# Seven block products for the down product of the last two FFN blocks, in place of whole tiles, with their output stored transposed

## The chip, the core and the metric

The kernel runs on one core of a Trainium2 chip. The metric is the device time of one execution in microseconds (us), as the median of several runs. Beside it stands one execution taken with the hardware profiler: its own time, the span from its first to its last instruction, and its trace. PE is TensorE, DVE VectorE, ACT ScalarE, POOL GpSimd, SP the engine that issues the DMAs.

## The reference

Attention with two kinds of masks over 4 batches gives 2304 tokens of width 512. A mixture of experts follows (MoE: 8 experts, each 512 to 1024 to 512, relu, gates from a Sinkhorn iteration), then an FFN (512 to 2048 to 512) whose activation is the sigmoid form of gelu. The change concerns the FFN alone:

```python
def _moe2_ref(x, w_in, w_out) -> np.ndarray:
    h = x @ w_in
    g = h * (1.0 / (1.0 + np.exp(-1.702 * h)))
    return (g @ w_out).astype(np.float32)
```

All matrices are float32. The kernel multiplies in a reduced format (fp32r) and keeps the precision by splitting each operand into a high and a low part: three matmuls (high by high, high by low, low by high) make one product.

## The kernel before

**Blocks, phases, units.** The tokens form three blocks of 768 (`BT`; half of one is `NH` = 384). There are six phases: MoE on blocks 0, 1, 2, then FFN on blocks 0, 1, 2. A phase is cut into units of 256 hidden columns: 32 units in a MoE phase, 8 in an FFN phase. Units are numbered through: 0 to 31, 32 to 63, 64 to 95 are the MoE phases, 96 to 103, 104 to 111, 112 to 119 the FFN phases. `S0` = 32 is the first unit of MoE block 1, `S1` = 96 the first FFN unit.

**Up product.** Each unit multiplies its token block by its 512x256 weights in a 2x2 block scheme with seven products instead of eight (Winograd's form; the table `PRODUCTS`). A product is six matmuls of 128x128 by 384 columns, so a unit has 42 of them. They go into PSUM banks A, B, C. ACT copies (`pB<-pA`, `c<-pC`, `c<-pA`) and DVE additions between the products finish the four quarters "11", "12", "21", "22" of the hidden block.

**Down product, by whole tiles.** In MoE block 0 and in all FFN blocks, `activate` makes for each quarter a high part `hh` and a low part `hl`. For the FFN that is a chain of four instructions: ACT sigmoid `sg`, DVE product `sg`, ACT copy `hh`, DVE difference `hl`. One unit later `tile_down` multiplies: six token tiles of 128, six matmuls of 512 columns each, 36 in a unit, and DVE adds each tile to the sums `acc`. Products and tiles alternate on PE. Quarter "12" comes from the last but one product of a unit and is wanted by the first tile in the next unit.

**Down product, by seven block products.** In MoE blocks 1 and 2 (`seven(i)`) the down product uses the same 2x2 scheme over a pair of units. `scaled` finishes a quarter `r`, `down_input_sum` forms four sums `s` on POOL, and `combination` and `low_part` split all seven inputs into high (ACT) and low parts in the tiles `comb`. The seven weight blocks come from DRAM (`sw7`, tiles `w7`), made once in MoE block 0. `chain` multiplies: 14 chains for a pair, each six matmuls of 384 columns, so 42 matmuls for a unit, two units later than the up products. DVE adds each chain to the sums `sums7`. The result is transposed (features by tokens), which is the form in which the FFN wants it.

**Weights.** The FFN weights come as 64-bit numbers and are decoded in the MoE phases (`plan_decode`). `plan_ahead` makes the sums and the split parts of three FFN units there already (its tiles are `ws`, its stores go to `s1ffn` and `s2ffn`). The other five units' parts are made while FFN block 0 runs, by ACT (high) and POOL (low), and stored for blocks 1 and 2.

**Order.** Everything is written in one order by hand: a unit is a row of pieces (product, down tile, product, ...), and lists of side work (`side`) hang on the pieces. Each engine executes its own instructions strictly in that order.

Of the kernel before, what the change touches and what calls it, by code (L numbers as in the profile page):

```python
# [15 lines left out]
P = 128  # L16
# [13 lines left out]
AHEAD = 3  # L30
# [27 lines left out]
def strided_attention_moe_ffn(  # L58
# [58 lines left out]
    sw2 = dram.tile([UF, 2, P, 2 * D], F32, name="s2ffn")  # L117
    sw7 = dram.tile([E * UPE, NPR, P, D], F32, name="s7moe")
# [168 lines left out]
    def split_w1(i, k):  # L287
# [20 lines left out]

    def split_w2(i, ft):
# [7 lines left out]
        kept = [(kept, f(t))] if kept is not None else []
        if kind == "moe":

            for k, (_, what, *_) in enumerate(PRODUCTS):  # L320
                if what[0] == "W" and int(what[1]) == ft + 1:
                    c = (int(what[2]) - 1) * D
                    kept.append((sw7[n, k], f(t)[:, c : c + D]))
# [1307 lines left out]
```

## Time and profile before

| what | value |
|---|---|
| median of 3 runs | 1961.44 us (1958.18 to 1962.76) |
| the profiled execution's own time | 1956.79 us |
| its span | 1955.0 us |
| PE busy | 1919.4 us, 98% of the span |
| DVE, ACT, POOL busy | 74%, 44%, 64% |
| granted PE clock, mean | 0.994 of full speed |
| DMA | 545.75 MB, 279 GB/s |

The profiled execution lies 4.65 us below the median of the runs, and its time is 1.8 us more than its span. Matmuls overlap each other in the profile, so a busy PE is not by itself a PE at its peak. What a stage costs is read from how many matmuls a stretch of it holds.

### The profile page before, as it was taken

How to read it: one execution, taken by the hardware profiler on the slowest of the kernel's cores; microseconds unless marked ns; L12 is line 12 of the kernel's file. 1: busy time of each engine (PE TensorE's matmuls, PEld its weight loads, DVE VectorE, ACT ScalarE, POOL GpSimd, SP SyncE). 2: the span in 40 equal slices, each digit the busy share in tenths (PEclk: the TensorE clock that was granted, in tenths of full speed). 3: DMA queues.
4: the chain of work that ended last, by engine and by line, in shares of the span. 5: the costliest groups of instructions: out<-in, count | busy, mean ns of one | idle time of the engine just before them, and what ended most of it. 6: DMA issues, size and time to landing. Idle time of an engine off the chain costs nothing.

```text
span 1955.0 us, 34399 instructions
## 1 busy us (share of the span) xinstructions
PE 1919.4 (98%) x11276; PEld 1793.0 (92%) x11276; DVE 1455.9 (74%) x2751; ACT 864.3 (44%) x2152; POOL 1242.0 (64%) x1249
## 2 busy tenths in 40 slices
PE   6999999999999999999999999999999999999999
PEld 5777888898888999999999999999999998888888
DVE  4787778777766788788878788888886766756555
ACT  4555556676665333333333433333333445533332
POOL 3456666777777677677777888888887767600100
PEclk8999999999999999999999999999999999999999
DMA  5457779999997898888898888999988867665653
GB/s 213 152 209 270 266 276 331 385 338 350 379 330 248 318 307 290 297 286 283 285 303 286 253 310 293 341 327 322 364 314 314 294 222 265 237 189 187 222 192 121
DMA packets 283649, 545.75 MB, mean 279 GB/s; under 512 B 30832, under 2 KB 51536, under 8 KB 282576
## 3 DMA queue, kind: packets, MB, share of 16 engines
q1 hardware_dynamic: 283184, 543.09, 80.5%
q8 instruction: 91, 1.49, 0.3%
q14 instruction: 86, 0.70, 0.1%
q10 hardware_dynamic: 288, 0.47, 0.1%
HBM read 381.90 MB, written 161.53 MB: 278 GB/s over the span
## 4 chain that ended last, share of the span: by engine, by line
PE 80%; DVE 2%; POOL 1%; ACT 0%; issue 0%; DMA 0%; ACTq 0%; DVEq 0%
PE y L1177 22%; PE pA L1017 22%; PE pC L1017 11%; PE y L1284 6%; PE y L1283 6%; PE y L1282 6%; PE pB L1017 5%; DVE xs L552 0%; POOL s L1149 0%; POOL comb L1124 0%; DVE comb L1124 0%; POOL xc L568 0%; DVE xc L572 0%; DVE r L1130 0%; DMA w<-s1moe 0%
## 5 line engine op out<-in xcount | busy, mean ns | idle before, releaser
L1017 PE MATMUL pA<-xc,w 128*128 128x384 f32 x2880 | 572.3, 336 | 1.9 <-DVE pB L1072 1.9
L1177 PE MATMUL y<-comb,w 128*128 128x384 f32 x2688 | 537.6, 334 | 1.4 <-DVE sum L1187 1.4
L1017 PEld LDWEIGHTS pA<-xc,w 128*128 128x128 f32 x2880 | 508.0, 188 | 18.8 <-DVE pB L1072 2.9
L1177 PEld LDWEIGHTS y<-comb,w 128*128 128x128 f32 x2688 | 472.0, 188 | 2.5 <-DVE sum L1187 2.4
L1124 POOL TENSOR_TENSOR comb<-s,comb 128x384 fp32r<-128x384 f32 x256 | 283.3, 1117 | 89.1 <-ACT comb L1119 82.4
L1187 DVE TENSOR_TENSOR sum<-y,sum 128x384 f32<-128x384 f32 x420 | 231.4, 552 | 98.5 <-PE y L1177 96.8
L1017 PE MATMUL pC<-xc,w 128*128 128x384 f32 x1464 | 295.0, 336 | 0.0
L1017 PEld LDWEIGHTS pC<-xc,w 128*128 128x128 f32 x1464 | 258.6, 188 | 10.0
L1284 PE MATMUL y<-w,hl 128*128 128x512 f32 x672 | 266.9, 397 | 0.4 <-DVE hl L1056 0.4
L1282 PE MATMUL y<-w,hh 128*128 128x512 f32 x672 | 263.4, 392 | 3.7 <-DVE acc L1297 2.0
L1283 PE MATMUL y<-w,hh 128*128 128x512 f32 x672 | 265.3, 395 | 0.0
L1119 ACT ACTIVATE comb<-r 128x384 fp32r<-128x384 f32 x192 | 101.0, 526 | 364.0 <-DVE r L1130 348.3
L252 POOL TENSOR_TENSOR w<-raw,w 128x512 fp32r<-128x512 f32 (+1 forms) x100 | 117.6, 1182 | 74.4 <-ACT w L258 69.9
L1284 PEld LDWEIGHTS y<-w,hl 128*128 128x128 f32 x672 | 125.9, 187 | 28.3 <-DVE hl L1056 1.0
L1282 PEld LDWEIGHTS y<-w,hh 128*128 128x128 f32 x672 | 126.2, 188 | 22.8 <-DVE acc L1297 2.6
L1017 PE MATMUL pB<-xc,w 128*128 128x384 f32 x708 | 142.4, 335 | 0.0
L1283 PEld LDWEIGHTS y<-w,hh 128*128 128x128 f32 x672 | 126.0, 187 | 15.9
L1124 POOL TENSOR_TENSOR comb<-r,comb 128x384 fp32r<-128x384 f32 x64 | 67.5, 1054 | 114.4 <-ACT comb L1119 114.4
L1119 ACT ACTIVATE comb<-s 128x384 fp32r<-128x384 f32 x256 | 131.5, 514 | 11.0 <-POOL s L1149 10.9
L1149 POOL TENSOR_TENSOR s<-r,r 128x384 f32<-128x384 f32 x127 | 134.8, 1082 | 2.1 <-DVE r L1130 2.0
L1311 DVE TENSOR_TENSOR acc<-y,acc 128x512 f32<-128x512 f32 x126 | 86.8, 689 | 63.3 <-PE y L1284 63.1
L1017 PEld LDWEIGHTS pB<-xc,w 128*128 128x128 f32 x708 | 125.2, 188 | 4.7
(178 smaller groups left out, 2878.0 us busy)
## 6 DMA issues: line engine op xcount, KB each, us to landing
w<-s1moe SPq DMA_DIRECT2D x448, 256.0 KB, 4.9
w<-s7moe SPq DMA_DIRECT2D x448, 256.0 KB, 4.9
s1moe<-w SPq DMA_DIRECT2D x216, 256.0 KB, 4.5
w<-s1ffn SPq DMA_DIRECT2D x133, 256.0 KB, 2.7
s7moe<-kw SPq DMA_DIRECT2D x116, 256.0 KB, 4.9
s7moe<-w SPq DMA_DIRECT2D x96, 256.0 KB, 4.7
w<-s2ffn SPq DMA_DIRECT2D x38, 512.0 KB, 3.7
raw<-wa SPq DMA_DIRECT2D x32, 512.0 KB, 5.9
```

The lines of the kernel that those rows point to most:

```text
L252: eng.tensor_tensor(out=t[:, 1], in0=src, in1=f(high), op=ALU.subtract)
L1017: nc.tensor.matmul(out=o, lhsT=w[:, hw, kk * P : (kk + 1) * P], rhs=x[:, hx, kk, :], start=opens and m == 0, stop=ends and m == len(todo) - 1,
L1119: nc.scalar.activation(out=t[:, 0, :], in_=part[i, q], func=AF.Copy)
L1124: eng.tensor_tensor(out=t[:, 1, :], in0=part[i, q], in1=f(t[:, 0, :]), op=ALU.subtract)
L1149: eng.tensor_tensor(out=part[i, q], in0=part[i, a], in1=part[i, b], op=op)
L1177: nc.tensor.matmul(out=o, lhsT=t[:, hw, dt * P : (dt + 1) * P], rhs=x[:, hx, :], start=(n == 0), stop=(n == 5))
L1187: nc.vector.tensor_tensor(out=a, in0=o, in1=a, op=ALU.add)
L1282: nc.tensor.matmul(out=o, lhsT=hh[:, c], rhs=w[:, 0], start=(m == 0), stop=False)
L1283: nc.tensor.matmul(out=o, lhsT=hh[:, c], rhs=w[:, 1], start=False, stop=False)
L1284: nc.tensor.matmul(out=o, lhsT=hl[:, c], rhs=w[:, 0], start=False, stop=(m == 1))
L1311: nc.vector.tensor_tensor(out=a, in0=y, in1=a, op=ALU.add)
```

## The change

FFN blocks 1 and 2 (units 104 to 119) get their down products by `chain` over pairs of units, as MoE blocks 1 and 2 have them. FFN block 0 keeps its tiles. `scaled` gets a branch for the FFN: ACT sigmoid `sg`, DVE product `r`. The sums of blocks 1 and 2 are joined and stored by `join_parts` and `store_part`, features by tokens, and the host puts the transposed part back. The weight blocks for this (`sw7["ffn"]`) are made for four units in the MoE phases (`AHEAD` = 4; two of them now in MoE block 1) and for the other four in FFN block 0, where their low parts and those of three of the seven up blocks go to DVE. On DVE the high part is staged, so ACT copies it twice. The whole-tile weights `sw2` are kept for the four early units alone.

```diff
-AHEAD = 3
+AHEAD = 4
...
+    F1 = FIRST_UNIT[NB + 1]
+    RANGES = ((S0, S1), (F1, NU))
 
     def seven(i):
-        return S0 <= i < S1
+        return any(lo <= i < hi for lo, hi in RANGES)
...
-            split_into(t, src, kept, store=2 if i > PLAIN else 0)
+            split_into(t, src, kept, nc.vector if kind == "ffn" and k % 2 else nc.gpsimd, store=2 if i > PLAIN else 0)
...
-        eng, tag = (nc.gpsimd, "sums") if again is None else (nc.vector, "psums")
+        ffn = UNITS[i][1] == "ffn"
+        eng, tag = (nc.gpsimd, "dsums" if ffn else "sums") if again is None else (nc.vector, "psums")
+        low = nc.vector if ffn else eng
+        last = i in (S0 - 1, F1 - 1)
...
-            split_into(t, src, sw7[n, k].rearrange("p (h c) -> p h c", h=2), eng, 1, 3)
+            split_into(t, src, sw7[UNITS[i][1]][n, k].rearrange("p (h c) -> p h c", h=2), low, 1, 3)
...
+            def down_sum(m, r=r):
+                w, t = r["raw"].rearrange("p (q c) -> p q c", q=4), r["sums"]
+                a, b = (
+                    (w[:, 1], w[:, 0]), (w[:, 3], w[:, 1]), (w[:, 3], t[:, 0, :]), (w[:, 2], t[:, 2, :])
+                )[m]
+                nc.gpsimd.tensor_tensor(out=t[:, m, :], in0=a, in1=b, op=ALU.subtract)
+
+            def split_down(k, m, r=r, n=n):
+                kept = sw7["ffn"][n, k].rearrange("p (h c) -> p h c", h=2)
+                src = r["sums"][:, WHERE[PRODUCTS[k][1]][1], :]
+                split_into(half_of(r, m).bitcast(F32R), src, kept, low=1, store=3)
...
+            tasks += [lambda m=m, down_sum=down_sum: down_sum(m) for m in range(4)]
+            tasks += [lambda k=k, m=m, fn=split_down: fn(k, m) for k, m in ((1, 0), (2, 1), (4, 0), (6, 1))]
+            tasks += [lambda: None] * 2
...
+        if UNITS[i][1] == "moe":
+            half = rows[UNITS[i][2], UNITS[i][3] // UPE][:, (int(q[0]) - 1) * NH : int(q[0]) * NH]
+            nc.vector.scalar_tensor_tensor(out=t, in0=src, scalar=0.0, in1=half, op0=ALU.max, op1=ALU.mult)
+        else:
+            sg = stp.tile([P, NH], F32, tag="sg", name="sg", bufs=2)
+            nc.scalar.activation(out=sg, in_=src, func=AF.Sigmoid, scale=1.702)
+            nc.vector.tensor_tensor(out=t, in0=src, in1=sg, op=ALU.mult)
...
+    def order_of(u):
+        return (0, 1, 2, 4, 5, 3, 6) if u == NU - 2 else tuple(range(NPR))
...
+    def store_part(ph, n, h):
+
+        half, dt = divmod(n, 2)
+        blk = UNITS[FIRST_UNIT[ph]][2]
+        o = out[blk * BT : (blk + 1) * BT, :].rearrange("t d -> (t d)").rearrange("(k p t) -> k p t", p=P, t=BT)
+        src = sum_of(ph, DOWN.index(PARTS[n]))[:, h, :]
+        nc.sync.dma_start(out=o[2 * dt + h, :, half * NH : (half + 1) * NH], in_=src)
+
+    def join_parts(ph, a, b, h, eng, stored=None):
+
+        o, x = (sum_of(ph, DOWN.index(q))[:, h, :] for q in (a, b))
+        eng.tensor_tensor(out=o, in0=o, in1=x, op=ALU.add)
+        if stored is not None:
+            store_part(ph, stored, h)
...
+            last = {
+                2: [(v, "12", "11", 0)],
+                3: [(g, "S4", "S1")],
+                4: [(v, "S2", "11"), (v, "S3", "S2"), (g, "S4", "S2")],
+                5: [(v, "22", "S3", 2), (g, "S1", "S3", 3)],
+            }
+            for k, steps in last.items():
+                side[piece_at(NU, k)] += [join(h, *step) for step in steps for h in range(2)]
...
-        plan_ahead(piece_at(FIRST_UNIT[2] + 5, 0), piece_at(S1 - 4, 0))
+        M2 = FIRST_UNIT[2]
+        ends = [(S0 + 11, S0 + 19), (S0 + 19, M2 - 4), (M2 + 5, M2 + 17), (M2 + 17, S1 - 4)]
+        plan_ahead([(piece_at(lo, 0), piece_at(hi, 0)) for lo, hi in ends])
...
-    return r.results[0]["y"]
+    y = r.results[0]["y"]
+    t = y[BT:].reshape(-1, _OUTS[0][1], BT).transpose(0, 2, 1)
+    return np.concatenate([y[:BT], t.reshape(-1, _OUTS[0][1])])
```

**PE, inside an FFN unit of block 2.** Before, one product (L1017) stands between two down tiles of six 512-column matmuls (L1282 to L1284); the numbers behind `w_`, `hh_` are buffers.

```order
L1282 MATMUL y<-w_23230,hh_23318 128x512
L1283 MATMUL y<-w_23230,hh_23318 128x512
L1284 MATMUL y<-w_23230,hl_23319 128x512
L1282 MATMUL y<-w_23254,hh_23274 128x512
L1283 MATMUL y<-w_23254,hh_23274 128x512
L1284 MATMUL y<-w_23254,hl_23275 128x512
L1017 MATMUL pA<-xc,w_23289 128x384 x6
```

Now a product (L1040) is followed by one chain (L1211), three matmuls for each unit of the pair:

```order
L1040 MATMUL pA<-xc,w_23699 128x384 x6
L1211 MATMUL y_23917<-comb_23623,w_23778 128x384 x3
L1211 MATMUL y_23917<-comb_23802,w_23778 128x384 x3
L1040 MATMUL pA<-xc,w_23763 128x384 x6
L1211 MATMUL y_23945<-comb_23623,w_23778 128x384 x3
L1211 MATMUL y_23945<-comb_23802,w_23778 128x384 x3
```

The 512-column matmuls are gone from units 104 to 119, and the two inputs of a chain (`comb`) belong to units that are one and two units older.

**ACT, across the end of unit 102 (FFN block 0).** These are the instructions from the fourth product's quarter "11" to quarter "12", before; `w` are split up-weights, `xc<-z` an input for the next block.

```order
L1061 ACTIVATE sg<-pB 128x384
L1063 ACTIVATE hh_20832<-sg 128x384
L258 ACTIVATE w_20838<-raw_20721 128x2x256
L258 ACTIVATE w_20851<-sums 128x256
L1061 ACTIVATE sg<-pB 128x384
L1063 ACTIVATE hh_20864<-sg 128x384
L258 ACTIVATE w_20880<-sums 128x256
L563 ACTIVATE xc<-z 128x768
L1061 ACTIVATE sg<-pC 128x384
L1063 ACTIVATE hh_20892<-sg 128x384
```

Now, from the fourth of these rows on:

```order
L259 ACTIVATE w_21004<-sums 128x256
L259 ACTIVATE kw<-dsums 128x256
L269 ACTIVATE high<-dsums 128x256
L1084 ACTIVATE sg<-pB 128x384
L1086 ACTIVATE hh_21020<-sg 128x384
L259 ACTIVATE kw<-dsums 128x256
L269 ACTIVATE high<-dsums 128x256
L259 ACTIVATE w_21040<-sums 128x256
L586 ACTIVATE xc<-z 128x768
L259 ACTIVATE kw<-dsums 128x256
L269 ACTIVATE high<-dsums 128x256
L1084 ACTIVATE sg<-pC 128x384
```

Three pairs `kw`, `high` (the new down-weight parts) stand between, two of them behind the sigmoid of quarter "22" and ahead of that of quarter "12".

**DVE, at the very end.** Before, the last rows are quarter "21" of the last unit and the additions of the last tiles:

```order
L1062 TENSOR_TENSOR sg<-pA,sg 128x384
L1311 TENSOR_TENSOR acc<-y,acc 128x512
L1066 TENSOR_TENSOR hl_23451<-sg,hh_23450 128x384
L1311 TENSOR_TENSOR acc<-y,acc 128x512 x5
L1627 UNCONDITIONAL_BRANCH
```

Now there are additions of chains (L1221, `sum<-y,sum`) and joins of two sums (L1238); each `y` is one chain.

```order
L1238 TENSOR_TENSOR sum_23040<-sum_23040 128x384 x2
L1221 TENSOR_TENSOR sum_23260<-y_24168,sum_23260 128x384
L1221 TENSOR_TENSOR sum_23260<-y_24176,sum_23260 128x384
L1221 TENSOR_TENSOR sum_23260<-y_24189,sum_23260 128x384
L1221 TENSOR_TENSOR sum_23260<-y_24197,sum_23260 128x384
L1238 TENSOR_TENSOR sum_23260<-sum_23260,sum_23040 128x384 x2
L1238 TENSOR_TENSOR sum_23040<-sum_23040,sum_23260 128x384 x2
L1221 TENSOR_TENSOR sum_23040<-y_24214,sum_23040 128x384
L1221 TENSOR_TENSOR sum_23040<-y_24222,sum_23040 128x384
L1238 TENSOR_TENSOR sum_23040<-sum_23040 128x384 x2
L1221 TENSOR_TENSOR sum_23260<-y_24238,sum_23260 128x384
L1221 TENSOR_TENSOR sum_23260<-y_24247,sum_23260 128x384
```

Of the last 14 chains, which follow each other on PE without a product between them, the first row stands between the additions of the sixth and the seventh. Four joins now stand between the additions of the tenth and the eleventh chain, and two more in front of the last two additions.

## Rows read from the trace of the kernel before

**Rows 1.** The page's head and part 1: busy us, share of the span, instructions.

```profile
span 1955.0 us, 34399 instructions
PE 1919.4 (98%) x11276; PEld 1793.0 (92%) x11276; DVE 1455.9 (74%) x2751; ACT 864.3 (44%) x2152; POOL 1242.0 (64%) x1249
```

**Rows 2.** Waits of PE from 315 us on: total us, times, longest.

```profile
PE pA L1017 <- DVE pB L1072: 1.9, 3, 1.0
PE y L1177 <- DVE sum L1187: 1.4, 3, 0.8
PE y L1282 <- ACT hh L1063: 1.1, 1, 1.1
PE ptr L989 <- DVE pr L980: 0.6, 1, 0.6
```

**Rows 3.** Stretches: length, busy us (instructions) of PE, PEld, DVE, ACT, POOL; clock, DMA, GB/s.

```profile
641.71:651.65 9.94, 9.94 (x67) 9.75 (x67) 3.82 (x8) 6.54 (x13) 6.76 (x7) 1.00 0.75 223
797.25:1044.77 247.52, 247.52 (x1429) 247.52 (x1429) 198.06 (x370) 80.16 (x172) 177.47 (x174) 1.00 0.90 292
1206.94:1265.18 58.24, 58.24 (x337) 58.24 (x337) 49.13 (x94) 21.30 (x49) 48.65 (x49) 1.00 0.93 333
1059.33:1075.14 15.81, 14.84 (x86) 14.52 (x86) 12.25 (x20) 5.65 (x12) 13.79 (x12) 1.00 0.75 250
1075.14:1090.46 15.32, 14.84 (x86) 14.52 (x86) 12.40 (x19) 7.67 (x14) 14.91 (x11) 1.00 0.71 193
1644.00:1659.64 15.64, 15.64 (x80) 14.06 (x80) 9.88 (x16) 8.09 (x20) 12.14 (x14) 1.00 0.89 338
1675.30:1692.70 17.40, 16.18 (x79) 13.90 (x79) 12.17 (x20) 11.71 (x23) 13.39 (x9) 1.00 0.59 201
1708.34:1770.90 62.56, 62.56 (x313) 56.22 (x313) 37.03 (x65) 21.64 (x44) 0.00 (x0) 1.00 0.62 197
```

**Rows 4.** Timeline of the last microseconds: start, us, engine, instruction, [idle before].

```profile
1950.92 0.39 PE L1284 MATMUL y<-w,hl 128*128 128x512 f32 x1
1951.34 0.69 DVE L1311 TENSOR_TENSOR acc<-y,acc 128x512 f32<-128x512 f32 x1 [0.67 <-PE y L1284]
```

**Rows 5.** Timeline of ACT across the end of unit 102.

```profile
1674.09 0.49 ACT L1061 ACTIVATE sg<-pB 128x384 f32<-128x384 f32 x1 [3.37 <-DVE pB L1072]
1675.20 0.53 ACT L1063 ACTIVATE hh<-sg 128x384 fp32r<-128x384 f32 x1 [0.62 <-DVE sg L1062]
...
1675.94 0.83 ACT L563 ACTIVATE xc<-z 128x768 fp32r<-128x768 f32 x1
1676.68 0.47 ACT L1061 ACTIVATE sg<-pC 128x384 f32<-128x384 f32 x1
```

**Rows 6.** Groups by form: count, busy us, mean ns of one, idle before.

```profile
L1187 DVE TENSOR_TENSOR sum<-y,sum 128x384 f32<-128x384 f32 x420 | 231.4, 552 | 98.5 <-PE y L1177 96.8
L258 ACT ACTIVATE kw<-dsums 128x256 fp32r<-128x256 f32 x116 | 47.3, 408 | 1.9 <-DMA s1moe<-kw 1.5 <-POOL dsums L343 0.2 <-DMA s7moe<-kw 0.2
L268 ACT ACTIVATE high<-dsums 128x256 fp32r<-128x256 f32 x12 | 4.5, 379 | 0.3
L252 DVE TENSOR_TENSOR kw<-dsums,high 128x256 fp32r<-128x256 f32 x12 | 5.0, 416 | 2.9 <-ACT high L268 1.4 <-POOL psums L235 0.5 <-issue 0.5
L252 POOL TENSOR_TENSOR ws<-ws 128x256 fp32r<-128x256 f32 x21 | 17.6, 838 | 0.0
L252 POOL TENSOR_TENSOR ws<-ws 128x512 fp32r<-128x512 f32 x6 | 8.3, 1382 | 0.0
```

**Rows 7.** Line L1208, joins of sums in SBUF: ns min/median/max, first and last start.

```profile
L1208 DVE TENSOR_TENSOR z<-sum x4: 548/862/900, 1111.4 to 1134.8; 128x384 f32<-128x384 f32 x4
L1208 DVE TENSOR_TENSOR sum<-sum,sum x4: 637/1108/1429, 1120.2 to 1127.7; 128x384 f32<-128x384 f32 x4
```

**Rows 8.** Waits of ACT from 600 to 1590 us: total, times, longest.

```profile
ACT ws L258 <- DMA s1ffn<-ws: 4.4, 2, 2.5
```

**Rows 9.** DMA issues by line: count, KB each, median us to landing.

```profile
s1ffn<-ws SPq DMA_DIRECT2D x21, 256.0 KB, 4.9
```

More of the change, by code (lines that the diff above doesn't have):

```diff
@@ L307, in halves, with blocks_of @@
         return src.rearrange("p (q c) -> p q c", q=2)
+    def blocks_of(ft):
+        return [
+            (k, int(what[2]) - 1)
+            for k, (_, what, *_) in enumerate(PRODUCTS)
+            if what[0] == "W" and int(what[1]) == ft + 1
+        ]
     def split_w2(i, ft):
@@ L312, in split_w2 @@
         w2[i, ft] = by_part(t)
-        kept = sw2[n, ft] if kind == "ffn" else None
         if not fresh(i):
-            nc.sync.dma_start(out=f(t), in_=kept)
+            nc.sync.dma_start(out=f(t), in_=sw2[n, ft])
             return
[L317 to L323, printed above, removed]
+        kept = [(sw7[kind][n, k], f(t)[:, c * D : (c + 1) * D]) for k, c in blocks_of(ft)]
         split_into(by_part(t), halves(raw[2, i][:, ft, :]), kept, low=(0, 2 - ft)[i >= PLAIN], store=(0, 4)[i >= PLAIN])
@@ L1366, in unit_pieces, with down @@
                 out.append(prod)
-            if k < TB or S0 + 2 <= i <= S1:
-                def down(i=i, k=k):
-                    if i == S1:
+            begin = next((lo for lo, hi in RANGES if lo <= i <= hi), None)
+            if k < TB or begin is not None and i >= begin + 2:
+                def down(i=i, k=k, begin=begin):
+                    if i in (S1, NU):
                         for c in (2 * k, 2 * k + 1):
-                            chain((S1 - S0) // 2 - 1, c)
-                    elif S0 + 2 <= i < S1:
-                        s, w = divmod(i - S0, 2)
-                        chain(s - 1, w * NPR + k)
-                    elif i == S0 + 1:
+                            chain(i - 2, c)
+                    elif begin is not None and i >= begin + 2:
+                        w = (i - begin) % 2
+                        chain(i - w - 2, w * NPR + k)
+                    elif begin is not None and i == begin + 1:
                         pass
@@ L1382, in down @@
                     after()
[L1383 removed]
+                if k < TB or i == NU:
                     out.append(down)
@@ L1539, in strided_attention_moe_ffn @@
         seven_pools.close()
-        raws = ctx.enter_context(ExitStack())
+        raws = ExitStack()
         rawp[0] = raws.enter_context(tc.tile_pool(name="rawf", bufs=1, reuse_waits="tile"))
+        for i in range(S1 + AHEAD, F1):
+            plan_down_sums(None, i)
+        while done[0] < piece_at(F1 - 1, 11):
+            advance()
+        raws.close()
+        sp[0] = ctx.enter_context(tc.tile_pool(name="sp2", bufs=1, reuse_waits="tile"))
         while done[0] < len(pieces):
```

109 lines of the change are left out of this document (65 added, 44 removed).

## The prediction

> **What bounds the kernel now.** I read the page first: PE is busy 98% of the span, the next engine (DVE) 74% [rows 1]. Busy PE alone proves little, so the second view is PE's waits. From 315 us to the end they come to 5.0 us in eight places [rows 2]: PE is fed, and the time is the number of matmuls times the time of one. The third view gives that time [rows 3]. In MoE block 1, 17 units of 84 matmuls of 384 columns take 247.52 us: 14.56 us a unit, 0.1732 us each. In FFN block 1, four units (42 such matmuls and 36 of 512 columns) take 62.56 us: 15.64 us a unit. The 36 therefore take 15.64 - 42 x 0.1732 = 8.37 us, 0.232 us each. That is 1.34 times a 384-column matmul for 1.33 times the columns, at clock 1.00 in both stretches (2.4 GHz). The columns cost, the count of instructions hardly.
>
> **The change part by part.**
>
> *PE's work.* A changed unit has 42 x 384 = 16,128 columns for its down product instead of 36 x 512 = 18,432. Its time goes from 15.64 to 14.56 us. From the start of unit 104 (1692.70 us) the old program has 16 units and the last six tiles (36 matmuls): 16 x 15.64 + 36 x 0.232 = 258.6 us, which ends at 1951.3, where the last matmul does end [rows 4]. The new one has unit 104 with the last tiles of block 0 (15.64), unit 105 with products alone (42 x 0.1732 = 7.28), 14 units of 14.56, and the last pair's 14 chains alone (14.56): 241.3 us. **-17.3 us**, and this term is sure: the 84-matmul unit ran 17 times without a gap.
>
> A rule speaks against it. The Trainium skill's "TensorE: Matmul & The Clock Gate", section "Back-to-back issue gap", gives about 81 ns a matmul at 128 columns and 131 ns at 512 in a stream of weight loads and matmuls, since weight loads set the spacing too; in between, on a straight line, 384 columns would cost about 114 ns (an estimate from that page). By it 42 x 114 = 4.8 us would replace 36 x 131 = 4.7 us, and this term would be +1 us in all. Here 384 columns take 173 ns and 512 take 232, nearly in proportion, so the rows decide.
>
> *Steady units 106 to 118.* The FFN form of `scaled` differs from the MoE form by one ACT sigmoid, about 0.5 us [rows 5], four times a unit. ACT is busy 80.16 of 247.52 us where the same scheme runs in MoE [rows 3], so 2 us more in 14.56 hides. POOL is at 72% there with the decoding. Cost 0. Chains read inputs one and two units old, so the tight path of the tile form (quarter "12" wanted two products later) is gone here.
>
> *Earlier weights, MoE phases.* An early unit now issues 20 POOL instructions instead of 12: 3 sums and 7 splits for the up weights, then 4 sums, 4 splits and the 2 large splits. At 0.84 us for a 256-wide one and 1.38 us for a 512-wide one [rows 6] that is about 18 us, where it was 12. Two such units now lie in some 17 units of MoE block 1: 36 us over 247.5 takes POOL from 72% to 86%. Block 2 carries 84% (48.65 of 58.24) and PE does not wait there [rows 3]. The DMAs: 1 MB loaded and 4.5 MB stored per early unit, 11 MB in 247 us, 45 GB/s on top of 292, against 333 in block 2's row and 338 in unit 101's. Cost 0; the bound is 4 us, from ACT waits on stores (below).
>
> *FFN block 0.* Each of units 100 to 103 gets four pairs `kw`, `high` on ACT (0.41 + 0.38 us), four DVE differences (0.42) [rows 6], and a second ACT copy for three up blocks. That is 4.3 us of ACT and some 3 us of DVE a unit. Unit 101 has 8.09 and 9.88 us of 15.64 [rows 3]: hidden. Unit 103 is the hard place. It makes the inputs of the next block too, has ACT at 11.71 and DVE at 12.17, and takes 17.40 us instead of 15.64 already [rows 3]. The reason is at the border of 102 and 103: ACT waits 3.37 us for a DVE addition that is late, so the sigmoid of quarter "12" comes at 1676.68 [rows 5] and PE waits 1.1 us for its high part and more for the low [rows 2]. In the new order three pairs are put into that stretch. The first falls into ACT's 3.37 us wait and is hidden. The two others (2 x 0.79 = 1.58 us) stand between that wait and the sigmoid of "12" and go to the path in full. DVE has differences ahead of the late addition: I add 0.4. In unit 103 ACT comes to 11.7 + 4.3 = 16.0 us, more than the unit's 15.6, so its "12" is late too: I add 1.0. Together **+3.0 us**. Lower bound 0 (all of it in idle time), upper 8.6 (two units of ACT's 4.3 us in full).
>
> *Entry into block 1 (unit 105).* Products follow each other without tiles between, so the banks turn round in 7.28 us. ACT has 14 instructions of about 0.5 us there (4 sigmoids, 3 bank copies, 7 high parts), and four times it waits some 0.62 us for DVE [rows 5]: 9.5 us, 2.2 too many. The MoE's entry, unit 33, takes 9.94 us with transposes between the products, and PE is busy for all of it [rows 3]. Bounds 0 and 3; I take **+1.2**.
>
> *Border of blocks 1 and 2.* The tile form crosses it without a wait. The seven-product form crossed the border of MoE blocks 1 and 2 in units of 15.81 and 15.32 instead of 14.56 [rows 3], PE behind DVE additions [rows 2], because DVE makes input sums and low parts there. The same lists hang on FFN units 110 and 111. 1.25 + 0.76 = **+2.0**; bounds 0 and 4.
>
> *The end.* Before, one DVE addition (0.69 us) follows the last matmul [rows 4], and the store follows that. Now the last 14 chains come 1.04 us apart (6 x 0.1732), and DVE's row is in the way. Let T be the end of the last matmul if nothing stalls. The tenth chain ends at T - 4.16, and its addition (0.55) at T - 3.6. Then come four joins, two additions, two joins and the two last additions: 6 joins of j and 4 x 0.55. So DVE ends at T - 1.4 + 6j. A join of two sums in SBUF takes 0.55 us at best, 0.86 and 1.11 in the medians, 1.43 at worst [rows 7]. With 0.86: T + 3.8, where it was T + 0.7. **+3.1 us**; 1.2 with the best, 6.5 with the worst. POOL's own last joins start after the eleventh addition and end before. PE stops for a bank in between, but ends before DVE. Stores before and after are of like size.
>
> The Trainium skill's "SBUF — State Buffer", section "Who interferes with whom", has a DVE instruction with two SBUF inputs and a GpSimd instruction that reads SBUF exclude each other for the whole instruction. By it each join would wait for a POOL instruction (at least 0.84 us [rows 6]) and take 1.4 us, and the end would cost 6.3 us (an estimate from that page's rule). Medians of 0.86 and 1.11 say that this happens to some of them.
>
> *Sum.* -17.3 + 3.0 + 1.2 + 2.0 + 3.1 = -8.0 us. The span goes from 1955.0 to 1947.0, the profiled execution's time from 1956.79 to 1948.8. That execution lies 4.65 us below the runs' median; from the median it is 1961.4 - 8.0 = **1953.4 us**.
>
> **The rivals.**
>
> *The drains cost next to nothing (chance 0.22).* ACT and DVE have 25% and more to spare on average, and PE passed most borders without a wait. Then only the end is paid, with the best joins: -17.3 + 1.2, 1945.3 us. Against it: the 1.8 us that unit 103 already loses.
>
> *The borders eat it (0.12).* The bounds together, with joins of 1.11 us at the end: 8.6 + 3 + 4 + 4.6 = 20 us against 17.3, so 1958 to 1965 us. For it: ACT at over 100% in unit 103. Against: the four places are short, and a stall in one gives the engines time to catch up.
>
> *Slower, by ACT standing behind stores in MoE block 1 (0.06).* The tiles `ws` are written again two tasks later. A unit's 30 tasks lie over 104 pieces now (before 20 over 100), so the next write is due 6.9 pieces after the last, and the store goes out 3 pieces after it. That leaves 3.9 pieces of 1.12 us, 4.4 us, for a store whose median is 4.9 [rows 9]. ACT then stands still with the bank copies behind it; it did so twice before, 2.5 us at most [rows 8]. PE bears about 2.4 us of that: a copy `pB<-pA` has a chain, a product and a chain (3.1 us) before the next product needs the bank, less 0.7 for itself. Some 19 such writes lie in block 1 (13 a unit, less the first few). Each wait would have to be 3.1 us (stores of 7.5 us) for 19 x 0.7 = 13 us to turn -8 into +5: 1966 us.
>
> *The matmul count decides (0.02).* If each matmul cost the same whatever its columns, 42 for 36 would cost 96 x 0.232 = 22 us more, with the 9.3 us of drains 1993 us. The two unit times in rows 3 speak against it. This is the direction in which the rule on issue gaps points.
>
> **How the numbers follow.** The forecast, with its chance of 0.58, spans 1949 to 1958 (the 9.3 us of drains at half and at one and a half times). No change can be told from this within about 0.2%, 3.9 us. Faster by more: the first rival and nearly all of the forecast, 0.22 + 0.55 = 0.77. Within: the forecast's upper edge and most of the second rival, 0.14. Slower: 0.09. The range reaches from the first rival less 1 us for the spread of the runs to the middle of the second, 1944.5 to 1961.5. It leaves out half of the second, the slower ones and a little below: 0.18.
>
> **What would show it.** Stretches: units 107 to 110 and 114 to 118 at 14.56 us, or else the first term is wrong. Unit 103 at 18 to 20 us, with PE waiting for ACT's `hh` or DVE's `hl` at down tiles. Units 110 and 111 with about 2 us of PE waits behind `pB`. The last DVE addition about 4 us after the last matmul would have ended unstalled, with joins of about 0.9 us in front. MoE units of blocks 1 and 2 unchanged at 14.56. Waits of PE in MoE block 1, or steady FFN units above 14.6, would make the prediction wrong; so would joins that run at 0.55 us and a unit 103 as before.

## The result and the profile after

The changed kernel takes 1971.93 us in the median (1969.74 to 1973.89, six runs), the kernel before 1959.59 us beside it: ratio 1.0064, 95% interval 1.0048 to 1.0080. It is 12.3 us slower where 8 us less were forecast. The profiled execution has a span of 1968.6 us, 13.6 us more than before. One of the six executions of e10 below took 2337.93 us at a granted clock of 0.749; the median given there is over all six, the ratio over the other five.

The page's head and part 1 answer to [rows 1]; PE's waits from 315 us on answer to [rows 2].

```profile
span 1968.6 us, 35350 instructions
PE 1913.5 (97%) x11372; PEld 1805.6 (92%) x11372; DVE 1475.4 (75%) x2787; ACT 898.7 (46%) x2260; POOL 1425.7 (72%) x1436
```

```profile
PE y L1363 <- DVE hl L1089: 4.9, 3, 2.4
PE pA L1040 <- DVE pB L1095: 4.6, 6, 1.2
PE y L1211 <- DVE sum L1221: 3.4, 3, 2.3
PE y L1211 <- DVE comb L1147: 2.8, 2, 1.9
PE y L1361 <- ACT hh L1086: 2.5, 3, 1.2
PE y L1211 <- DMA w<-s7ffn: 1.5, 1, 1.5
PE y L1211 <- DMA w<-s7moe: 1.4, 1, 1.4
PE pC L1040 <- DVE r L1154: 1.1, 1, 1.1
```

PE's busy time fell by 5.9 us, and its waits rose from 5.0 to over 22 us. Every wait has its place. The view by stretches (length, busy time, clock, DMA, as in [rows 3]) shows MoE units 33 to 63, then 50 and 56; FFN units 100 to 105; 106 to 109; 110 with 111; and 116:

```profile
644.00:1100.10 456.10, 449.09 (x2587) 446.17 (x2587) 368.93 (x655) 160.91 (x345) 362.99 (x354) 1.00 0.91 312
...
886.90:903.52 16.62, 15.15 (x85) 14.51 (x85) 14.56 (x24) 7.32 (x16) 13.25 (x13) 1.00 0.99 356
...
979.32:996.14 16.82, 14.92 (x86) 14.48 (x85) 12.32 (x23) 5.29 (x12) 14.28 (x15) 1.00 1.04 312
1637.66:1653.30 15.64, 15.64 (x80) 14.05 (x80) 9.58 (x19) 10.71 (x28) 10.82 (x14) 1.00 0.52 182
1653.30:1670.39 17.09, 15.93 (x79) 14.00 (x79) 11.22 (x24) 11.78 (x31) 9.77 (x11) 1.00 0.87 318
1670.39:1691.18 20.79, 17.99 (x80) 15.39 (x80) 15.44 (x26) 10.62 (x28) 16.60 (x17) 0.92 0.69 236
1691.18:1711.53 20.35, 17.77 (x79) 15.25 (x79) 12.95 (x24) 13.26 (x31) 15.82 (x12) 0.92 0.72 250
1711.53:1728.68 17.15, 16.20 (x79) 13.92 (x79) 12.24 (x21) 8.07 (x16) 4.07 (x3) 1.00 0.69 225
1728.68:1737.41 8.73, 7.57 (x43) 7.25 (x43) 3.59 (x6) 4.29 (x10) 6.87 (x7) 1.00 0.95 316
1737.41:1795.65 58.24, 58.24 (x337) 58.24 (x337) 32.09 (x62) 27.87 (x61) 39.10 (x38) 1.00 0.84 274
1795.65:1826.36 30.71, 29.50 (x169) 29.08 (x169) 22.28 (x36) 15.20 (x30) 27.41 (x22) 1.00 0.76 245
1884.60:1901.05 16.45, 14.97 (x85) 14.50 (x85) 7.87 (x15) 7.66 (x18) 11.21 (x12) 1.00 1.04 375
```

Read against a unit without stalls, or against the kernel before, the balance of the two profiled executions is:

| place | predicted | after less before, us |
|---|---|---|
| fewer columns on PE | -17.3 | -17.3 (four units in 58.24 = 4 x 14.56, no gap) |
| MoE block 1, units 33 to 63 | 0 | +7.4 (456.10 against 448.75): units 50, 52, 56 at 16.62, 17.56, 16.81 |
| FFN block 0, units 96 to 104 | +3.0 | +11.0 (161.40 against 150.35) |
| unit 105 | +1.2 | +1.5 |
| units 110, 111 | +2.0 | +1.6 |
| unit 116 | not seen | +1.9 |
| the end | +3.1 | +5.6 |

The sum is +11.7. The rest of the 13.6 us is +2.3 ahead of unit 33, where the change puts nothing, and -0.3 in MoE block 2. Unit 33 starts between 640.2 and 647.1 us in the profiles of this document, so the +2.3 is spread between executions.

Two rows of the balance have a spread of their own, since further kernels below leave the same stage as it is in the changed kernel. Units 33 to 63 take 455.96 to 459.93 us in the changed kernel and five others (e2, e5, e6, e8, e11), units 96 to 104 take 158.62 to 161.40 us in it and five others (e3, e4, e7, e8, e12). So the two losses are 7.2 to 11.2 and 8.3 to 11.0 us, and a difference within that spread is not an effect.

At the end, the DVE timeline (start, us, instruction, count, idle before) answers to [rows 4]; the two groups of joins below it, by engine (ns least/median/most), to [rows 7]:

```profile
1955.35 0.56 DVE L1221 TENSOR_TENSOR sum<-y,sum 128x384 f32<-128x384 f32 x1 [0.48 <-PE y L1211]
1955.82 4.43 DVE L1238 TENSOR_TENSOR sum<-sum,sum 128x384 f32<-128x384 f32 x4
1960.17 1.01 DVE L1221 TENSOR_TENSOR sum<-y,sum 128x384 f32<-128x384 f32 x2
1961.10 2.38 DVE L1238 TENSOR_TENSOR sum<-sum 128x384 f32<-128x384 f32 x2
1963.41 1.01 DVE L1221 TENSOR_TENSOR sum<-y,sum 128x384 f32<-128x384 f32 x2
```

```profile
L1238 POOL TENSOR_TENSOR sum<-sum x4: 1007/1160/1319, 1954.0 to 1958.5; 128x384 f32<-128x384 f32 x4
L1238 DVE TENSOR_TENSOR sum<-sum,sum x4: 598/1350/1361, 1955.8 to 1958.9; 128x384 f32<-128x384 f32 x4
```

### The profile page after: what moved, and what is told of

Same layout as the page of the kernel before. It is cut to its first block, busy times and chain, and to the rows that moved or that the text cites. A ratio compares the mean times of both kernels' runs of the same rounds, so it can differ in the third digit from the quotient of the medians.

```text
span 1968.6 us, 35350 instructions
## 1 busy us (share of the span) xinstructions
PE 1913.5 (97%) x11372; PEld 1805.6 (92%) x11372; DVE 1475.4 (75%) x2787; ACT 898.7 (46%) x2260; POOL 1425.7 (72%) x1436
## 4 chain that ended last, share of the span: by engine, by line
PE 65%; DMA 6%; DVE 4%; POOL 3%; issue 2%; ACT 1%; SPq 0%; DVEq 0%; POOLq 0%; ACTq 0%
PE y L1211 25%; PE pA L1040 18%; PE pC L1040 9%; PE pB L1040 5%; PE y L1363 3%; PE y L1362 3%; PE y L1361 3%; DMA w<-s7moe 2%; DMA s1moe<-w 1%; POOL s L1177 1%; DVE xs L575 1%; DMA rows<-prd 1%; DVE comb L1147 1%; DMA s7ffn<-ws 1%; POOL comb L1147 0%
## 5 line engine op out<-in xcount | busy, mean ns | idle before, releaser
L1211 PE MATMUL y<-comb,w 128*128 128x384 f32 x3360 | 670.7, 334 | 9.0 <-DVE sum L1221 3.4
L1211 PEld LDWEIGHTS y<-comb,w 128*128 128x128 f32 x3360 | 589.4, 188 | 12.0 <-DVE sum L1221 4.3
L1040 PE MATMUL pA<-xc,w 128*128 128x384 f32 x2880 | 574.8, 336 | 5.0 <-DVE pB L1095 4.6
L1040 PEld LDWEIGHTS pA<-xc,w 128*128 128x128 f32 x2880 | 507.1, 188 | 19.3 <-DVE pB L1095 7.2
L1147 POOL TENSOR_TENSOR comb<-s,comb 128x384 fp32r<-128x384 f32 x320 | 353.4, 1115 | 93.6 <-ACT comb L1142 87.1
L1221 DVE TENSOR_TENSOR sum<-y,sum 128x384 f32<-128x384 f32 x504 | 276.2, 550 | 117.5 <-PE y L1211 115.5
L1040 PE MATMUL pC<-xc,w 128*128 128x384 f32 x1464 | 297.1, 337 | 1.1 <-DVE r L1154 1.1
L1040 PEld LDWEIGHTS pC<-xc,w 128*128 128x128 f32 x1464 | 259.8, 189 | 8.8 <-DVE r L1154 1.4
L1363 PE MATMUL y<-w,hl 128*128 128x512 f32 x480 | 192.0, 400 | 5.6 <-DVE hl L1089 4.9
L1361 PE MATMUL y<-w,hh 128*128 128x512 f32 x480 | 189.8, 395 | 4.7 <-ACT hh L1086 2.5
L1362 PE MATMUL y<-w,hh 128*128 128x512 f32 x480 | 190.3, 396 | 0.0
L1040 PE MATMUL pB<-xc,w 128*128 128x384 f32 x708 | 142.3, 335 | 0.0
L1147 DVE TENSOR_TENSOR comb<-r,comb 128x384 fp32r<-128x384 f32 x160 | 118.4, 740 | 16.7 <-ACT comb L1142 11.2
L1040 PEld LDWEIGHTS pB<-xc,w 128*128 128x128 f32 x708 | 124.9, 188 | 3.4
L1380 DVE SCALAR_TENSOR_TENSOR acc<-y,pr,acc 128x512 f32<-128x512 f32 x114 | 85.2, 747 | 53.5 <-PE y L1363 53.3
L1095 DVE TENSOR_TENSOR pC<-pC,c 128x384 f32<-128x384 f32 x118 | 66.6, 565 | 76.2 <-ACT c L1066 75.7
L1363 PEld LDWEIGHTS y<-w,hl 128*128 128x128 f32 x480 | 90.5, 189 | 27.5 <-DVE hl L1089 6.6
```

The source lines that it names most:

```text
L1040: nc.tensor.matmul(out=o, lhsT=w[:, hw, kk * P : (kk + 1) * P], rhs=x[:, hx, kk, :], start=opens and m == 0, stop=ends and m == len(todo) - 1,
L1095: nc.vector.tensor_tensor(out=o, in0=bank[b][:, :NH], in1=t, op=ALU.add)
L1147: eng.tensor_tensor(out=t[:, 1, :], in0=part[i, q], in1=f(t[:, 0, :]), op=ALU.subtract)
L1211: nc.tensor.matmul(out=o, lhsT=t[:, hw, dt * P : (dt + 1) * P], rhs=x[:, hx, :], start=(n == 0), stop=(n == 5))
L1221: nc.vector.tensor_tensor(out=a, in0=o, in1=a, op=ALU.add)
L1361: nc.tensor.matmul(out=o, lhsT=hh[:, c], rhs=w[:, 0], start=(m == 0), stop=False)
```

## Experiments

Theory: the columns are saved, and three places give them back, each through a queue: ACT and SP in MoE block 1, ACT and DVE in FFN block 0, DVE at the end. Rivals: the products save nothing; the amount of work (or of DMA) is too much wherever it stands. Each median is given beside one of the kernel before that was measured with it. The edits are those against the changed kernel, cut to the parts of lines that matter; `...` stands for what is left out.

**e1: the products alone**

```diff
-AHEAD = 4
+AHEAD = 3
...
-        for i in range(S1 + AHEAD, F1):
-            plan_down_sums(None, i)
...
-in_=sw7[kind][n, OF[DOWN[j]]]
+in_=sw7["moe"][n, OF[DOWN[j]]]
...
```

> The seven products of FFN blocks 1 and 2 alone: weights are prepared as in the kernel before (three early units, whole-tile weights stored), and the FFN's chains read the MoE's down blocks instead, so the output of blocks 1 and 2 is another function with the same number and size of loads. Theory (the columns are saved and the engines around give it back): 1959.6 - 17.3 + 1.5 (unit 105) + 1.6 (111) + 1.9 (116) + 5.6 (end) = 1953 us, MoE block 1 at 14.56 a unit, units 101 to 104 at 15.64, 15.67, 17.40, 15.64. Rival (the products themselves, or their loads from DRAM, cost as much as the tiles did): about 1960 us or more, FFN units above 14.56.

Measured: 1951.15 against 1958.68, ratio 0.9972 (0.9962 to 0.9983). MoE block 1 takes 448.73 us, FFN block 0 150.33, all as before. Units 105, 110, 111 and 116 are over by 1.5, 0.8, 1.3 and 2.0, and the end costs what it costs in the changed kernel: 1955.0 - 17.3 + 5.6 + 5.6 = 1948.9 us, and the span is 1948.8. The saving is real; the borders and unit 116 give back 5.6 us of it and the end 5.6. What the changed kernel loses beyond that comes with the weights.

**e2: without the new parts in FFN block 0**

```diff
-nc.vector if kind == "ffn" and k % 2 else nc.gpsimd, store=2
+store=2
...
-        for i in range(S1 + AHEAD, F1):
-            plan_down_sums(None, i)
...
-in_=sw7[kind][n, OF[DOWN[j]]]
+in_=sw7[kind][n if kind == "moe" else n % AHEAD, OF[DOWN[j]]]
```

> In FFN block 0 the down sums and their split parts are left out and the low parts of the up blocks go back to POOL; chains of FFN units 4 to 7 read the blocks of units 0 to 3 (output of blocks 1 and 2 changed). Everything else as in the changed kernel. Theory (these parts alone make units 101 to 104 late): units 101 to 104 back at 15.64, 15.67, 17.40, 15.64, 11.0 us less than 1971.9, 1961 us. Rival (the stores of the blocks to DRAM or the early work keeps them late): 1968 to 1972 us.

Measured: 1963.39 against 1958.68, ratio 1.0022 (1.0013 to 1.0031). Units 96 to 104 take 150.39 us (101 to 104: 15.64, 15.68, 17.41, 15.64). The 11.0 us come with these parts and with the low parts that the change moved from POOL to DVE. (The median fell by only 8.5 us: in this profile units 33 to 63 took 458.00 us and unit 116 18.88.)

**e3: without the down parts in the MoE phases**

```diff
-            tasks += [lambda m=m, down_sum=down_sum: down_sum(m) for m in range(4)]
-            tasks += [lambda k=k, m=m, fn=split_down: fn(k, m) for k, m in ((1, 0), (2, 1), (4, 0), (6, 1))]
-            tasks += [lambda: None] * 2
...
```

> In the MoE phases the four early units get no down sums and no split down parts (20 tasks a unit in the same stretches instead of 30); chains of FFN units 0 to 3 read the blocks of units 4 to 7 (output of blocks 1 and 2 changed). Theory (the denser tasks cost units 50, 52 and 56): MoE block 1 at 14.56 in every unit but the border ones, 7.4 us less, 1964.5 us. Rival (two early units in block 1 are too many even without the down parts): 2 to 4 us less, 1968 to 1970 us.

Measured: 1965.79 against 1958.68, ratio 1.0032 (1.0020 to 1.0044). Units 33 to 63 take 448.99 us: two early units in block 1 are not too many; their down parts, and the closer spacing of the tasks that they bring, cost the 7 us. (Unit 92, in block 2, took 18.33 us in this profile, at most 15.15 in the others. PE waited 1.9 us there for `w<-s7moe`; what held that load is open.)

**e4: a later rewrite of the halves of `ws`**

```diff
-((1, 0), (2, 1), (4, 0), (6, 1), (0, 2), (3, 3), (5, 0))
+((1, 0), (4, 1), (2, 2), (6, 0), (0, 1), (3, 3), (5, 2))
...
-((1, 0), (2, 1), (4, 0), (6, 1))
+((1, 0), (4, 1), (2, 2), (6, 0))
```

> The complete changed kernel, with another order of the blocks of an early unit: each half of the tile ws is written again three tasks after the last time at the least, not two (10.4 pieces of about 1.12 us instead of 6.9). Same instructions, bytes and engines. Theory (ACT stands behind the store of what it is to write over): unit 50 back at 14.56, ACT's waits on stores gone in MoE block 1, 52 and 56 better or as they are: 1965 to 1970 us. Rival (POOL at 86% is late and holds SP's queue): unchanged within 0.1%, 1971 to 1973 us.

Measured: 1965.99 against 1958.68, ratio 1.0052 (1.0032 to 1.0071). Unit 50 is at 14.56. ACT's waits on stores from 640 to 1100 us, in the changed kernel (they answer to [rows 8]),

```profile
ACT ws L259 <- DMA s7ffn<-ws: 11.1, 3, 4.8
ACT ws L259 <- DMA s1ffn<-ws: 4.1, 3, 2.7
```

are in e4 down to

```profile
ACT ws L259 <- DMA s7ffn<-ws: 0.3, 1, 0.3
```

Units 52 and 56 stay late, at 19.29 and 16.99, so the whole stretch is no shorter (455.93 us against 456.10): the lower median can't be put down to this edit. In these two units PE waits for the loads `w<-s7moe`. SP's queue says what those loads stood behind (e4, 900 to 1010 us):

```profile
SPq L257 <- POOL ws L253: 8.4, 3, 4.4
...
SPq L451 <- DMA s7ffn<-ws: 4.0, 1, 4.0
```

The last row is the load that opens the second early unit (L451), waiting for the stores of the first; the other is stores waiting for POOL's low part. SP issues in the written order, so the loads behind them went out late.

**e7 and e12: the two waits of SP, together and one alone**

e7 is e4 with

```diff
-(S0 + 19, M2 - 4)
+(S0 + 20, M2 - 4)
...
-kept, low=1, store=3)
+kept, low=1, store=5)
```

and e12 is e4 with the first of the two edits alone.

> The complete changed kernel with e4's order of blocks; besides, an early unit's stores are issued five pieces after the copy instead of three, and the second early unit starts one unit later than the first one ends. Theory (in units 52 and 56 SP stood behind ws: at the start of the second early unit for the stores of the first, 4.0 us, and behind a store that waited for POOL's low part, 3.4 to 4.4 us, and the loads of the down blocks came late): all of MoE block 1 at 14.56 but the border, 448.9 us for units 33 to 63 instead of 456.1, 1964.6 us. Rival (the DMA engines are too full there for the loads, whatever the order of issue): 52 and 56 stay late, 1969 us.

> e4's order of blocks and the second early unit one unit later, but stores three pieces after the copy as in the changed kernel: e7 without its later stores. Theory (unit 52 was the handover from the first early unit to the second, unit 56 a store that waited for POOL): 52 at 14.56, 56 (or the unit in which that store now lies, one later) still 2 us late; units 33 to 63 451 us, 1967 us. Rival (the gap is enough, POOL was late only because of the handover): 448.8 us, 1964.5 us.

Measured, e7: 1960.59 against 1958.91, ratio 1.0007 (0.9996 to 1.0019); units 33 to 63 in 448.73 us, PE without a wait from 850 to 1000 us. e12: 1963.19 against 1958.33, ratio 1.0021 (1.0009 to 1.0034); 451.11 us, unit 52 at 14.56, unit 56 at 16.78. So 52 was the handover and 56 the store behind POOL. The row of e7 for the same stretch,

```profile
640.24:1088.97 448.73, 447.31 (x2587) 446.48 (x2587) 372.12 (x655) 161.57 (x345) 363.40 (x354) 1.00 0.92 317
```

has the instructions and the busy times of the first row of stretches above (POOL 363.40 and 362.99): the same work, 7.4 us less. All of the loss is gone with e4's order and the two edits together; e7 without e4's order was not run, so how much of it the waits of ACT alone were worth is open.

**e5: the new FFN units earlier**

```diff
+FFN_ORDER = (0, 1, 2, 4, 5, 6, 7, 3)
...
-        for n in range(E * UPE if kind == "moe" else UF):
+        for n in range(E * UPE) if kind == "moe" else FFN_ORDER:
...
```

> The complete changed kernel with the FFN's units in another order: the four whose weights are made in FFN block 0 come as units 99 to 102, and unit 103 has one with early weights. Same work. Theory (ACT and DVE are too full where unit 102 and 103 also make the next block's inputs): unit 103 back at 17.4 or less (its own stall of 1.8 was there before for the same reason, and may go), 99 to 102 at about 17 each as unit 101 was (1.45 over), so 150.35 + 5 for units 96 to 104 against 161.4: 6 us less, 1966 us. Rival (the coupling of ACT and DVE costs the same wherever it is put): 161 us in the stretch, 1972 us.

Measured: 1975.26 against 1958.91, ratio 1.0081 (1.0068 to 1.0094). Units 96 to 104 take 161.37 us, the changed kernel 161.40: the theory that the border with the next block's inputs makes the loss fell. Unit 103, which now makes no parts of its own, took 22.88.

**e6: one copy instead of two**

```diff
-        if late and eng is nc.vector:
+        if late and eng is nc.vector and twice:
...
```

> The complete changed kernel, but the low parts that DVE makes in FFN block 0 read the high part from the SBUF tile itself; ACT's second copy of each (0.38 us, seven a unit, 2.7 us) is gone. Theory (ACT's work, and DVE's waits for the second copy, hold the units up): units 101 to 104 come to 68 us instead of 75.4, 4 to 7 us less, 1965 to 1968 us. Rival (a DVE instruction with two inputs in SBUF takes turns with POOL, 1.35 us instead of 0.42, as the joins at the end of e1 did): seven times 0.9 us a unit, DVE past 15.6 us, 5 to 15 us more, 1977 to 1987 us.

Measured: 1969.59 against 1958.91, ratio 1.0054 (1.0037 to 1.0071). Units 96 to 104 take 158.55 us; five kernels that leave this stage alone (e3, e4, e7, e8, e12) have 160.3, 159.8, 160.9, 158.6 and 158.95. Inconclusive: neither the gain nor the rival's loss is seen.

**e9, e10, e11: another place for the split down parts**

What ACT and DVE did at the end of unit 101 and the start of 102 in the changed kernel gave the next theory. Their timelines, 1669 to 1676 us (they answer to [rows 5]):

```profile
1669.22 0.40 ACT L259 ACTIVATE kw<-dsums 128x256 fp32r<-128x256 f32 x1
1669.53 0.39 ACT L269 ACTIVATE high<-dsums 128x256 fp32r<-128x256 f32 x1
1669.86 0.47 ACT L1084 ACTIVATE sg<-pC 128x384 f32<-128x384 f32 x1
1672.14 0.52 ACT L1086 ACTIVATE hh<-sg 128x384 fp32r<-128x384 f32 x1 [1.81 <-DVE sg L1085]
```

```profile
1669.08 0.42 DVE L253 TENSOR_TENSOR kw<-dsums,high 128x256 fp32r<-128x256 f32 x1 [1.59 <-ACT high L269]
1669.41 0.68 DVE L1390 TENSOR_TENSOR acc<-y,acc 128x512 f32<-128x512 f32 x1
1670.01 1.30 DVE L1089 TENSOR_TENSOR hl<-sg,hh 128x384 fp32r<-128x384 f32 x1
1671.23 0.41 DVE L253 TENSOR_TENSOR kw<-dsums,high 128x256 fp32r<-128x256 f32 x1
1671.57 0.54 DVE L1085 TENSOR_TENSOR sg<-pC,sg 128x384 f32<-128x384 f32 x1
1673.28 0.42 DVE L253 TENSOR_TENSOR kw<-dsums,high 128x256 fp32r<-128x256 f32 x1 [1.17 <-ACT high L269]
1673.62 0.68 DVE L1390 TENSOR_TENSOR acc<-y,acc 128x512 f32<-128x512 f32 x1
1674.22 1.78 DVE L1089 TENSOR_TENSOR hl<-sg,hh 128x384 fp32r<-128x384 f32 x1
```

```profile
1673.79 1.79 POOL L575 TENSOR_TENSOR xs<-xs,z 128x768 f32<-128x768 f32 x1
```

Quarter "12" (`sg<-pC`) is what the next down tile needs. ACT has its sigmoid done at 1670.3, but DVE's product comes at 1671.57: DVE had stood 1.59 us for a `high` copy, and two `kw` differences are ahead of it. ACT then stands 1.81 us, so the next `high` is late, and DVE stands 1.17 us for that before the `hl` of "12". Each engine waits for the other through the parts put between the steps of "12". The last `hl` takes 1.78 us instead of 0.55, beside a POOL sum of 1.79.

e10 is e5, e7 and e8 (below; one pair of joins stays on POOL) together, with the parts after "12" instead of ahead of it, and a second buffer for the down sums; in e9 they stand at pieces 11 to 14, with one buffer; e11 is the changed kernel with e10's two lines alone, except for unit 103.

```diff
-at = piece_at(i, (7, 4)[last] + m)
+at = piece_at(i, (11, 12, 15, 17)[m] if ffn else (7, 4)[last] + m)
...
-tag=tag, name="dsums")
+tag=tag, name="dsums", bufs=2 if ffn else 1)
```

> The complete changed kernel with e5's order of units, e7's MoE block 1 and e8's end (POOL takes the join of 12 with 11 alone); new is that in FFN block 0 the four split down parts of a unit are issued after its quarter 12 (pieces 11, 12 and the first two of the next unit) and not in front of it (pieces 7 to 10). Theory (it is the place in the queues of ACT and DVE, in front of the sigmoid chain of quarter 12, for which the next unit's first down tile waits, and not the amount of work): units 100 to 103 at 15.64 to 16, 151 to 153 us for units 96 to 104 instead of 161; with block 1 (-7.2), unit 116 (-1.9) and the end (-2) 1972 - 9 - 11 = 1952 us. Rival (ACT and DVE are too full, wherever the parts stand): about 159 us in that stretch, 1960 us.

> As e9, but the four parts lie at pieces 11 and 12 and at the third and fifth piece of the next unit, and the down sums have a second buffer, so that they need not be done before the next unit's sums. Theory of the place in the queues: 151 to 152 us for units 96 to 104, at least as good as e9, whose first two pieces of a unit also hold three copies of up blocks; 1951 us. Rival (amount of work): about 159 us, 1960 us.

> The changed kernel with nothing altered but the place of the split down parts of units 100 to 102 (pieces 11 and 12, and the third and fifth of the next unit, with a second buffer of the down sums); the order of units is the changed kernel's, and unit 103 keeps its parts where they were. Theory (the place in the queues is the whole cause; the order of the units adds nothing): units 101 to 103 at 15.64, 15.67, 17.4 to 19, unit 104 at 17.1 because unit 103 keeps its place: 152 to 154 us for units 96 to 104 instead of 161.4, 1963 us. Rival (it needs both, since unit 103 also makes the next block's inputs): units 102 and 103 stay over 18 us each, 157 us or more, 1968 us.

Measured: e9 1951.09 against 1957.29, ratio 0.9962 (0.9950 to 0.9974), units 96 to 104 in 152.24 us. e10 **1946.39** against 1957.29, ratio **0.9938** (0.9925 to 0.9951), 149.53 us. e11 1965.90 against 1958.33, ratio 1.0041 (1.0025 to 1.0057), 156.31 us, with unit 101 at 15.64, 102 and 103 at 17.66 and 19.92. So in units 96 to 104 order alone gives nothing (e5). Both together give 9.1 to 11.9 us against the 158.62 to 161.40 of the kernels that leave the stage alone. Place alone (e11) gives 2.3 to 5.1, and its 156.31 lies between what the theory and the rival expected: while unit 103 has parts of its own, they can't be moved behind its "12", since their pool closes there. Units 101 to 103 in e10:

```profile
1645.30:1660.94 15.64, 15.64 (x80) 14.06 (x79) 12.72 (x23) 11.19 (x31) 11.11 (x12) 1.00 0.87 323
1661.00:1676.60 15.60, 15.60 (x79) 13.96 (x78) 13.75 (x24) 8.25 (x21) 10.90 (x10) 1.00 0.93 323
1676.60:1693.20 16.60, 16.23 (x80) 13.94 (x79) 13.23 (x22) 12.11 (x26) 10.28 (x6) 1.00 0.76 260
```

PE does not wait in the first two, and 0.4 us in the third. The rows of the whole stage, units 96 to 104, first in the changed kernel, then in e10:

```profile
1567.28:1728.68 161.40, 152.87 (x751) 136.56 (x751) 108.73 (x190) 83.31 (x193) 90.37 (x86) 0.98 0.67 229
1559.20:1708.73 149.53, 148.14 (x752) 134.08 (x751) 110.31 (x190) 83.08 (x193) 91.94 (x87) 1.00 0.73 247
```

DVE and ACT have as many instructions in both, and the same busy time within 2%. The amount of work was not the cause. Nor were slow differences `hl` beside POOL: 10 of the stage's 32 last over 0.7 us in the changed kernel, 13 in e10.

**e8: the joins on DVE**

```diff
-                2: [(v, "12", "11", 0)],
-                3: [(g, "S4", "S1")],
-                4: [(v, "S2", "11"), (v, "S3", "S2"), (g, "S4", "S2")],
-                5: [(v, "22", "S3", 2), (g, "S1", "S3", 3)],
+                2: [(v, "12", "11", 0), (v, "S2", "11")],
+                3: [(v, "S4", "S1")],
+                4: [(v, "S3", "S2"), (v, "S4", "S2")],
+                5: [(v, "22", "S3", 2), (v, "S1", "S3", 3)],
...
-            store_part(ph, stored, h)
+            after_pieces(0 if ph == 2 * NB - 1 else 4, lambda: store_part(ph, stored, h))
```

> The complete changed kernel; at the end all joins go to DVE, none to POOL, and the join of sum S2 with 11 is done before the last chain of S2; the stores of block 1's joined sums are issued four pieces after the join. Theory (DVE and POOL took turns over the joins, 1.35 us each; alone a join takes 0.5 us): the last DVE addition 2 us after the unstalled end of PE instead of 5, and unit 116 without its stall of 1.9: 5 us less, 1967 us. Rival (joins of two SBUF inputs are slow by themselves, and DVE has now 14 instead of 8): the end 2 to 5 us later than in the changed kernel, 1972 to 1975 us.

Measured: 1968.44 against 1958.91, ratio 1.0041 (1.0028 to 1.0054). Unit 116 is at 14.56. In the changed kernel SP had stood there behind stores of block 1's joined sums that waited for POOL (1830 to 1900 us):

```profile
SPq L1233 <- POOL sum L1238: 9.7, 2, 5.5
```

Of this edit only the later stores concern block 1; SP's longest such wait falls to 3.7 us. (Units 33 to 63 took 459.93 us in this profile, so the median shows less than the gain.) DVE ends 4.35 us after the unstalled end of PE instead of 5.13, and the span ends 1.7 us earlier against that mark, where 3 us were expected. The joins (ns least/median/most):

```profile
L1238 DVE TENSOR_TENSOR sum<-sum x8: 541/544/1369, 1951.6 to 1961.2; 128x384 f32<-128x384 f32 x8
L1238 DVE TENSOR_TENSOR sum<-sum,sum x6: 540/545/1361, 1953.4 to 1962.1; 128x384 f32<-128x384 f32 x6
```

Away from POOL a join takes 0.54 us; two of the first three, beside POOL's work, take 1.36 and 1.37. But there are 14, and DVE goes without a pause from 1951.6 on: now the count is the limit. e10 gives one pair to POOL and has DVE's end at 3.34.

## Why the prediction was wrong

Two steps failed: FFN block 0 was priced by busy time, and the early weights in the MoE phases were put at nothing. The end was mis-sized, and unit 116 was not seen.

*PE's work, -17.3:* right, to 0.1 us, and e1 shows it alone. The rule of the Trainium skill's "TensorE: Matmul & The Clock Gate", section "Back-to-back issue gap", that was weighed against it does not hold here: with it (+1, and e1's 11.2 us at the borders and the end) e1 would be some 12 us slower than the kernel before, and it is 7.5 us faster.

*FFN block 0, +3.0:* wrong, 11.0 (8.3 at least, see the spread above), where the text called 8.6 the upper bound. The failing step compared ACT's and DVE's busy time with the length of a unit ("hidden" in unit 101, at 8.09 and 9.88 of 15.64). Unit 101 took 17.09 all the same. What counted was where the parts stood in two in-order queues that wait for each other. The border of units 102 and 103, which the text took as the one hard place, was only part of it: units 101 to 104 lost 1.45, 5.1, 3.0 and 1.5 us. The text never costed DVE's stands for `high`. The bound (ACT's 4.3 us twice) is none for a wait: e10 does the same work, and this stage takes 0.8 us less than in the kernel before.

*Early weights in the MoE phases, 0:* wrong, 7.4. The mechanism of the "slower" rival was there: ACT stood 15.2 us behind stores in six waits, 2.5 us each. PE bore the 2.1 us of unit 50. The other 5.3 (7.2 in e4, where ACT's waits are gone) came from a queue that the text did not go through, SP's: stores that wait for POOL, and the load that opens the second early unit, hold the loads behind them. The share of POOL was forecast well. In the 17 units for which the text gave 86% it was busy for 84% of the changed kernel's time:

```profile
799.54:1054.44 254.90, 249.29 (x1430) 247.21 (x1429) 205.12 (x370) 88.92 (x198) 214.35 (x214) 1.00 0.93 322
```

e7 has the same 214 instructions of POOL there, 214.11 us of 247.52, and no unit is late. What failed is the step from that share to "cost 0": a store issued three pieces after the copy met a POOL that was still behind, and SP stood with everything behind it.

*Unit 105, +1.2, and units 110 and 111, +2.0:* right in place and cause (PE `pA` behind DVE `pB`), measured 1.5 and 1.6. *Steady units 106 to 118 at no cost:* right but for unit 116, 1.9, SP again.

*The end, +3.1:* right place, mis-sized: 5.6. The term took 0.86 us a join from the median of rows with other neighbours. The six joins took 0.60 to 1.36 us each, since POOL joins at the same time, and moved DVE on by 1.1 us a join (4.35 for four, 2.31 for two). So DVE's end cost 4.4 (5.13 after the unstalled end of PE against 0.7). By the Trainium skill's "SBUF — State Buffer", section "Who interferes with whom", the text had estimated 6.3 for it, with 1.4 a join. Four of the six single joins are near that price (1.34 to 1.36), the whole lies between the forecast and the rule. The other 1.2 of the 5.6 is a term put at nothing ("stores before and after are of like size"): the stores behind the last addition take 4.2 us instead of 3.0.

The four sizes missed (8.0, 7.4, 2.5 and 1.9) are 19.8 us. Taken from +11.7, they leave -8.1, the forecast. (Two small slips do not move it: an old early unit's 12 us of POOL are 11.2 by the text's own prices, and 14.56 / 84 is 0.1733, not 0.1732.) e7 and e8 undo the second and part of the rest, e10 all of the first.

## What to carry to other kernels

Busy shares do not price work put into in-order queues: list, for each engine and for SP, what stands just ahead of the chain that PE waits for next, and place new work behind that chain. A store whose producer is late is a wait for every load behind it on the same queue, so issue it when the producer is surely done, and leave time between the last store of a buffer and the load that opens it again. Where DVE reads two inputs from SBUF while POOL works, take both durations from rows where the two engines overlap.

## What the runs showed of the hardware

DVE and POOL hold each other up when both read from SBUF. A join is 0.54 us with POOL idle (e8); of the eight joins on DVE in the changed kernel, all beside POOL's work, five take 1.34 us or more. POOL's 1.01 becomes 1.31 to 1.32. Additions with one input in PSUM stay at 0.55 in either case.

A stall can cost more than itself. In unit 102 PE stood 0.43 us for `hh` and then, two matmuls later, 2.37 us for `hl`. Behind that its granted clock was

```profile
1676.65:1679.40 2.75, 2.75 (x9) 2.58 (x8) 2.05 (x4) 2.40 (x7) 2.59 (x4) 0.50 1.06 407
```

that is 1.2 GHz, and 512-column matmuls came 0.427 us apart instead of 0.232. In units 102 and 103 of the changed kernel 16 matmuls ran at such a pace, 2.5 us of the 11.0; in that stage of e10 none did. Not every stall does this: in unit 52 of e4 PE stood 2.05 us and, after some 9 us of work, 1.81 us, and the clock behind them stayed at 1.00. What made the difference was not tested.
